# Weight blocks 8 to 11 as two pieces: splitting one step of a float64 unpacking in a Mamba-2 and gated MLP kernel

## The chip, the cores and the metric

The kernel runs on one core of a Trainium2 chip. A core has five engines that run their own instruction streams: TensorE (PE, with its weight loads shown as PEld), VectorE (DVE), ScalarE (ACT), GpSimd (POOL) and SyncE (SP), and 16 DMA engines that move data between HBM and the on-chip memories. The metric is the device time of one execution, in microseconds (us), as the median of several runs.

## What is computed

```python
# attention: batch 4, 8 heads, 768 steps in chunks of 32, head_dim 32, d_state 16
la  = log(clip(a, 1e-6, 1));  cum = cumsum(la) within a chunk
L   = exp(cum[i] - cum[j]) * causal
y   = ((C B^T) * L) x  +  (C state) * exp(cum)
state = exp(sum la) * state + sum_j B_j x_j exp(cum_end - cum_j)
# MLP: 3072 tokens, d_model 256, d_ff 2048; w_in and w_out are float64
h = x @ w_in;  g = h / (1 + exp(-1.702 h));  out = g @ w_out
```

The heads' outputs, side by side, are the tokens of the MLP. All activations are float32. The two weight matrices come as float64, and the chip has no float64 arithmetic, so the kernel turns each word pair into a float32 with integer and float operations on VectorE and ScalarE.

## The kernel before, in words

The 3072 tokens are worked in six groups of 512. For the first group the kernel computes the attention part of two pairs of chunks, then `hidden(0, f)` for the 16 blocks of 128 columns of w_in (line 878), then the projection with w_out in 16 steps (`project_all`, line 976). Later groups use seven-product matrix schemes (lines 934, 944, 1039, 1046), for which VectorE forms sums of weights and of activations.

While the first group runs, the weights are still being loaded and unpacked. `PIECES` (line 155) lists the units of that work: pieces 0 to 3 are two blocks of w_in each (0 and 1, 2 and 3, 4 and 5, 6 and 7), piece 4 is blocks 8 to 11, piece 5 is blocks 12 to 15, and pieces 6 to 9 are four blocks of w_out each. A piece goes through these steps:

- `fetch(i)` (line 164): two DMA transfers on SP into a tile `bits`. Two-block pieces share a tile by twos. There are four such tiles; `NEXT` (line 214) and the schedule say after which join a tile is fetched into again.
- `fields(i)` (lines 193 and 196, VectorE): exponent field `p` and mantissa `m` out of the high words. It waits for the piece's transfers.
- `clamp(i)` (lines 204 and 205, ScalarE): the exponent in float32's range.
- `rounded(i)` (line 209, VectorE): the low word added to the mantissa.
- `join(i, parts)` (lines 223 and 229, VectorE): sign and exponent, then the product into `w_in` or `w_out`. It waits for the clamp. With two parts each half of the piece is done by its own pair of instructions.

`narrow(i)` (line 236) chains these for one piece: `rounded(i)`, then `join(i)` either ahead of `fields(i + 1)` or behind it. `m` and `p` have two buffers each, so at most two pieces are between fields and join.

The order on each engine is the order in which the program is written (`in_order`, line 1409, holds the instructions to it). The table at line 1221 sets behind which hidden block `narrow(i)` and `clamp(i + 1)` are written; `at` (line 1208) adds other work behind hidden blocks or ahead of projection steps: clipping the decays (`store_a` with `az`, line 1213; `clip_rows` with `af`, line 488), `decay_rows` (line 504), the loads of later pairs, `turn` (transposes into a bank `tp`, line 579, and `since_start`, line 649, which multiplies one half of `tp` into `CsT`), and ahead of projection step 10 `score` (line 664) and `gain` (the matmuls A, line 695). PSUM banks come from a ring of four (`bank`, line 563).

Of the kernel before, what the change touches and what calls it, by code (L numbers as in the profile page):

```python
# [35 lines left out]
def kernel(  # L36
# [48 lines left out]
    PG = CG // 2  # L85
# [31 lines left out]
    def load_blocks(p, queues=(nc.sync, nc.sync)):  # L117

        g, n = divmod(p, PG)
        b, c = divmod(2 * p, NC)  # L120
        for queue, name, src in zip(queues, "CB", (C, B)):
            if n == 0:
                blocks[name, g] = raw.tile([P, 2, PG * P], FP32, tag="z", name=f"z{name}{g}", bufs=2)
            for r in range(R):
                queue.dma_start(
                    out=blocks[name, g][32 * r:32 * r + 32, :, n * P:(n + 1) * P],
                    in_=src[b, Q * r:Q * r + Q, c * P:(c + 2) * P].rearrange(
                        "q (i f) n -> i q (f n)", i=32))
# [10 lines left out]
    def load(p, parts=None):  # L139
        if parts is None:  # L140
            parts = "bcx" if p < 2 * PG else "bx"
            if p >= 2 * PG:
                load_blocks(p)
        for part in parts:
            dst, src, e = {"b": (rb, B, N), "c": (rc, C, N), "x": (rx, x, D)}[part]
            dst[p] = raw.tile([P, 2, NH, e], FP32, tag=part, name=f"{part}{p}",
                              bufs=2 if part == "c" else 3)
            for k in range(2):
                b, c = divmod(2 * p + k, NC)
                sl = slice(c * P, (c + 1) * P)  # L150
                nc.sync.dma_start(out=dst[p][:, k], in_=src[b, :, sl, :].rearrange("h s d -> s h d"))


    assert NF == 4 * CG
    PIECES = [("in", f, 2) for f in range(0, 8, 2)] + [("in", 8, 4), ("in", 12, 4)] \
        + [("out", f, 4) for f in range(0, NF, 4)]
    PN = 4 * DM
    BUFS = 4
    bits, pieces = {}, {}

    def words(name):
        return wide.tile([P, 2 * PN], U32, tag="bits", name=name, bufs=BUFS)

    def fetch(i, held=False):
        name, f, n = PIECES[i]
        if n == 2 and f % 4:
            t = pieces.pop(i - 1)[:, 2 * n * DM:]
        else:
            t = pieces[i] = words(f"bits{i}")
            t = t[:, :2 * n * DM]  # L170
        if held:
            held.memset(t[:, :1], 0)
        if name == "in":
            src = moe_w_in[:, 2 * f * P:2 * (f + n) * P].rearrange("(k p) e -> p k e", p=P)
            dst, src = (v.rearrange(s, h=n, e=2 * P) for v, s in (
                (t, "p (h k e) -> k p h e"), (src, "p k (h e) -> k p h e")))
        else:
            src = moe_w_out[f * P:(f + n) * P, :].rearrange("(f p) (h e) -> h p f e", p=P, h=2)
            dst = t.rearrange("p (h f e) -> h p f e", h=2, f=n)
        for k in range(2):  # L180
            nc.sync.dma_start(out=dst[k], in_=src[k])  # L181
        t = t.rearrange("p (e w) -> p e w", w=2)
        bits[i] = t[:, :, 0], t[:, :, 1]
# [3 lines left out]
    mantissa, power = {}, {}  # L187

    def fields(i):
        hi, cols = bits[i][1], slice(0, PIECES[i][2] * DM)  # L190
        mantissa[i] = wide.tile([P, PN], U32, tag="m", name=f"m{i}")[:, cols]
        power[i] = wide.tile([P, PN], U32, tag="p2", name=f"p2{i}")[:, cols]
        nc.vector.tensor_scalar(out=power[i], in0=hi, scalar1=0x7FF00000, scalar2=None,
                                op0=ALU.bitwise_and)

        nc.vector.tensor_scalar(out=mantissa[i], in0=hi, scalar1=0x000FFFFF,
                                scalar2=0x00100000, op0=ALU.bitwise_and, op1=ALU.bitwise_or)

    def clamp(i):


        e = power[i]
        z = e.bitcast(FP32)
        nc.scalar.activation(z, e, AF.Relu, scale=-8.0, bias=edge[:, 0:1])
        nc.scalar.activation(e, z, AF.Relu, scale=-1.0, bias=edge[:, 1:2])

    def rounded(i):

        nc.vector.scalar_tensor_tensor(out=mantissa[i].bitcast(FP32), in0=bits[i][0],
                                       scalar=2.0 ** -32, in1=mantissa[i],  # L210
                                       op0=ALU.mult, op1=ALU.add)


    NEXT = {1: (6,), 5: (9,)}

    def join(i, parts=1):

        name, f, n = PIECES[i]
        n //= parts
        low, m, p2 = bits.pop(i)[1], mantissa.pop(i), power.pop(i)  # L220
        for k in range(parts):
            cols, fs = slice(k * n * DM, (k + 1) * n * DM), slice(f + k * n, f + (k + 1) * n)
            nc.vector.scalar_tensor_tensor(out=p2[:, cols], in0=low[:, cols], scalar=0x80000000,
                                           in1=p2[:, cols], op0=ALU.bitwise_and, op1=ALU.bitwise_or)
            if name == "in":
                dst, h = w_in[:, fs].rearrange("p f k e -> p (f k e)").unsqueeze(1), 1
            else:
                dst, h = w_out[:, :, fs].rearrange("p c f e -> p c (f e)"), 2
            nc.vector.scalar_tensor_tensor(  # L229
                out=dst, in0=m[:, cols].bitcast(FP32).rearrange("p (h e) -> p h e", h=h),  # L230
                scalar=2.0 ** -20, in1=p2[:, cols].bitcast(FP32).rearrange("p (h e) -> p h e", h=h),
                op0=ALU.mult, op1=ALU.mult)
        for n in NEXT.get(i, ()):
            fetch(n)

    def narrow(i):
        rounded(i)
        if i in (2, 4, 5, 6):
            join(i, 2 if i in (4, 5) else 1)
        if i == 6:  # L240
            decay_rows(0)
        if i + 1 < len(PIECES):
            fields(i + 1)
        if i not in (2, 4, 5, 6):
            join(i, 2 if i == 3 else 1)


    scratch = dram.tile([NC, 2, NB * NH, H], FP32, name="scratch")
# [133 lines left out]
    for n in range(PG):  # L382
        t = whose[32 * n:32 * n + 32, n:n + 1]
# [115 lines left out]
    def decay_rows(b):  # L499

        t, first = raf.pop(b), firsts.pop(b)
        if b:
            since[b] = ssd.tile([P, NC, P], FP32, tag="since", name=f"since{b}")
        nc.vector.tensor_tensor_scan(
            out=since[b][:, -t.shape[1]:].rearrange("p c s -> p (c s)"), data0=t.rearrange("p c s -> p (c s)"),
            data1=first.rearrange("p c s -> p (c s)"),
            initial=0.0, op0=ALU.mult, op1=ALU.add)
# [51 lines left out]
    def turn(p):  # L559
        turn_only(p)  # L560
        since_start(p)
# [81 lines left out]
    def since_start(p, engine=nc.vector):  # L643

        b, c = divmod(2 * p, NC)
        s = st[p]
        tp = s["tp"]
        s["CsT"] = ssd.tile([P, 2, P], FP32, tag="CsT", name=f"CsT{p}", bufs=3)
        engine.tensor_tensor(out=s["CsT"], in0=tp, in1=since[b][:, c:c + 2], op=ALU.mult)  # L649
# [79 lines left out]
    def keep_both(pairs, by_scalar=False):  # L729

        for p in pairs:
            part_of(p, range(4), by_scalar)
        for p in pairs:
            add_up(p, range(4))
# [448 lines left out]
    parts_first()  # L1183
    since_start(0, nc.gpsimd)
    fetch(1, held=nc.gpsimd)
    for i in range(2, 6):
        fetch(i)
    nc.sync.dma_start(out=az[:BH].rearrange("p c s -> p (c s)"),
                      in_=a.rearrange("b h s -> (b h) s"))
# [18 lines left out]
    def at(places, i, *work):  # L1208
        places.setdefault(i, []).extend(work)

    in_hidden = [{} for _ in range(NG)]
    in_project = [{} for _ in range(NG)]
    def store_a():
# [1 line left out]
        for i, side in enumerate(SIDES):  # L1215
            nc.sync.dma_start(out=scratch[:, i].rearrange("c r i -> r c i"), in_=az[:BH, :, side])

    at(in_hidden[0], 5, store_a, lambda: fetch(7), lambda: fetch(8),
       lambda: load(PG + 1, "bc"))
    at(in_hidden[0], 8, lambda: clip_rows(0))  # L1220
    for i, k, c in ((2, 1, 1), (3, 2, 2), (4, 4, 7), (5, 8, 10), (6, 10, 14), (7, 14, 15)):
        at(in_hidden[0], k, lambda i=i: narrow(i))
        at(in_hidden[0], c, lambda i=i: clamp(i + 1))
    at(in_hidden[0], 15, lambda: decay_fanned(PG))
# [1 line left out]
       lambda: load(PG, "x"), lambda: load(PG + 1, "x"))  # L1226
    n, p = 2 * PG, 3 * PG
    pairs = PG, PG + 1
    at(in_project[0], 0, lambda: turn(PG), lambda: rounded(8),
       lambda: join(8), lambda: fields(9))  # L1230
    at(in_project[0], 1, lambda: clamp(9))
    at(in_project[0], 2, lambda: clip_rows(1), lambda: decay(PG + 1),
       lambda: decay_rows(1))
    at(in_project[0], 4, lambda: turn(PG + 1))
    at(in_project[0], 5, lambda: narrow(9))
    at(in_project[0], 10, lambda: score(pairs), lambda: gain(pairs), lambda: keep_both(pairs, True),
       lambda: weigh(PG), lambda: weigh(PG + 1))
    at(in_project[0], 15, lambda: finish(pairs))
# [89 lines left out]
    k = NF // 2 - 1  # L1328
# [6 lines left out]
    for g in range(2, NG):  # L1335
        n, p = (g + 1) * PG, (g + 2) * PG
# [60 lines left out]
        k = NF // 2 - 1  # L1397
# [42 lines left out]
```

## Time and profile before

| quantity | value |
|---|---|
| median of 3 runs | 346.89 us (346.83 to 347.21) |
| the profiled execution's own time | 347.67 us |
| its span, first to last instruction of the program | 345.9 us |
| TensorE busy | 339.2 us (98%) |
| VectorE busy | 256.1 us (74%) |
| ScalarE busy | 155.1 us (45%) |
| GpSimd busy | 16.7 us (5%) |
| granted TensorE clock | 1.00 |
| share of the chain that ended last: TensorE, DMA | 92%, 3% |

The busy shares are means over the span. The chain that ended last goes back from the last instruction to whatever released each step. A timeline row gives start, duration, engine, line, operation, output and inputs, shapes and, in brackets, how long the engine stood idle before it and what ended that. "x24" merges 24 instructions in a row. A matmul of 512 columns is two records of 0.43 us each.

The rows of the first 90 us matter here, where the hidden blocks and the projection of the first group run beside the unpacking. Busy time by engine in some stretches:

| stretch, us | length | PE | DVE | ACT | share of the DMA engines |
|---|---|---|---|---|---|
| 24.0 to 29.5 | 5.5 | 4.67 | 4.30 | 3.68 | 1.10 |
| 29.5 to 34 | 4.5 | 4.48 | 4.40 | 3.38 | 0.80 |
| 34 to 42 | 8 | 8.00 | 7.84 | 5.45 | 0.77 |
| 42 to 50 | 8 | 8.00 | 7.40 | 5.97 | 1.00 |
| 50 to 58 | 8 | 8.00 | 7.93 | 2.89 | 1.07 |
| 58 to 66 | 8 | 8.00 | 7.80 | 3.30 | 0.60 |
| 82 to 90 | 8 | 8.00 | 7.14 | 4.55 | 0.54 |

### The profile page before, as it was taken

What the parts mean: (1) busy time and instruction counts of PE and PEld (TensorE: products, weight loads), DVE (VectorE), ACT (ScalarE), POOL (GpSimd) and SP (SyncE); (2) the same over time, 40 slices, a digit from 0 to 9 for tenths busy, and PEclk for the clock granted to TensorE, in tenths of its full rate; (3) what the DMA queues carried; (4) which work ended last, traced back from release to release, by engine and by line L of the source; (5) the groups of instructions that cost most, each with busy time, mean ns of one, the idle gap of its engine ahead of it and who ended that gap; (6) DMA issues with size and microseconds to landing.
All of it is one profiled execution on the core that took longest, in us unless ns stands there. A gap on an engine that the chain in (4) does not pass through costs nothing.

```text
span 345.9 us, 8116 instructions
## 1 busy us (share of the span) xinstructions
PE 339.2 (98%) x3380; PEld 270.2 (78%) x3380; DVE 256.1 (74%) x484; ACT 155.1 (45%) x352; POOL 16.7 (5%) x40
## 2 busy tenths in 40 slices
PE   8999999999999999999999999999999999999996
PEld 6633744555788888888888888888888888899996
DVE  5988999999799998858995667787564654465463
ACT  5786771507454324754332554442454322554320
POOL 7300110300000100000000000000000000000000
PEclk9999999999999999999999999999999999999999
DMA  6698899545637100435603036400000300000401
GB/s 160 132 289 211 217 239 133 152 67 102 122 63 127 36 0 15 65 99 100 110 27 51 2 78 121 64 0 3 0 4 2 62 2 0 0 2 0 63 0 62
DMA packets 90004, 25.76 MB, mean 74 GB/s; under 512 B 73416, under 2 KB 87248, under 8 KB 89968
## 3 DMA queue, kind: packets, MB, share of 16 engines
q1 hardware_dynamic: 89104, 24.72, 35.0%
q10 hardware_dynamic: 832, 0.52, 0.5%
q8 instruction: 26, 0.43, 0.5%
q14 instruction: 10, 0.08, 0.1%
q0 software_dynamic: 32, 0.01, 0.0%
HBM read 22.00 MB, written 3.24 MB: 73 GB/s over the span
## 4 chain that ended last, share of the span: by engine, by line
PE 92%; DMA 3%; SPq 2%; DVE 1%; issue 0%; ACT 0%; POOL 0%; DVEq 0%
PE acc L1039 28%; PE X L934 19%; PE Y L944 14%; PE o L976 8%; PE acc L1046 7%; PE h L878 7%; DMA bits<-in_moe_w_in_dram 3%; PE y L818 2%; PE cb L664 2%; SPq L181 1%; PE y L804 1%; PE A L695 1%; PE ab L536 1%; DMA az<-in_a_dram 1%; POOL CsT L649 0%
## 5 line engine op out<-in xcount | busy, mean ns | idle before, releaser
L939 ACT ACTIVATE ac<-X 128x256 f32<-128x256 f32 x76 | 29.1, 383 | 81.7 <-PE X L934 81.0
L1039 PE MATMUL acc<-mg,mw 128*128 128x256 f32 x192 | 54.5, 379 | 0.0
L1066 DVE TENSOR_TENSOR gT<-Y,ac 128x512 f32<-128x512 f32 x38 | 26.2, 689 | 38.1 <-PE Y L944 32.5
L911 ACT ACTIVATE gT<-gT 128x512 f32<-128x512 f32 (+1 forms) x76 | 38.9, 519 | 29.3 <-DVE gT L1066 28.8
L934 PE MATMUL X<-my,mi 128*128 128x256 f32 x152 | 45.2, 380 | 0.0
L1039 PEld LDWEIGHTS acc<-mg,mw 128*128 128x128 f32 x192 | 36.6, 190 | 4.9
L1066 DVE TENSOR_TENSOR gT<-Y,b 128x256 f32<-128x256 f32 x38 | 15.8, 419 | 28.5 <-PE Y L944 28.5
L878 PE MATMUL h<-yT,w_in 128*128 128x512 f32 (+1 forms) x92 | 35.5, 541 | 1.4 <-DVE w_in L229 0.9
L1039 PE MATMUL acc<-gT,w_out 128*128 128x256 f32 x128 | 35.5, 380 | 0.0
L878 PEld LDWEIGHTS h<-yT,w_in 128*128 128x128 f32 x92 | 17.2, 190 | 18.2 <-issue 12.8
L934 PEld LDWEIGHTS X<-my,mi 128*128 128x128 f32 x152 | 28.0, 190 | 4.0 <-ACT ac L939 0.3
L976 PE MATMUL o<-gT,w_out 128*128 128x512 f32 x64 | 28.3, 596 | 0.0
L902 DVE TENSOR_TENSOR mg<-gT 128x512 f32<-128x512 f32 x40 | 27.2, 681 | 0.0
L1039 PEld LDWEIGHTS acc<-gT,w_out 128*128 128x128 f32 x128 | 24.3, 190 | 3.4 <-ACT yT L853 0.2
L939 ACT ACTIVATE b<-X 128x256 f32<-128x256 f32 x38 | 14.6, 383 | 20.8 <-PE X L934 20.3
L934 PE MATMUL X<-yT,w_in 128*128 128x256 f32 x76 | 23.2, 389 | 0.0
L944 PE MATMUL Y<-yT,w_in 128*128 128x256 f32 x76 | 22.7, 381 | 0.0
L944 PE MATMUL Y<-my,mi 128*128 128x256 f32 x76 | 22.7, 381 | 0.0
L934 PE MATMUL X<-my,w_in 128*128 128x256 f32 x76 | 22.5, 380 | 0.0
L944 PE MATMUL Y<-yT,mi 128*128 128x256 f32 x76 | 22.5, 380 | 0.0
L976 PEld LDWEIGHTS o<-gT,w_out 128*128 128x128 f32 x64 | 11.9, 190 | 13.6 <-issue 12.7
L408 DVE TENSOR_TENSOR_SCAN L<-a,idents 128x1024 f32<-128x1024 f32 x9 | 20.5, 2279 | 0.3 <-DMA a<-scratch 0.3
(152 smaller groups left out, 547.8 us busy)
## 6 DMA issues: line engine op xcount, KB each, us to landing
a<-scratch SPq DMA_DIRECT2D x18, 256.0 KB, 4.9
bits<-in_moe_w_out_dram SPq DMA_DIRECT2D x8, 512.0 KB, 7.4
x<-in_x_dram SPq DMA_DIRECT2D x24, 128.0 KB, 3.7
out_dram<-ob SPq DMA_DIRECT2D x40, 64.0 KB, 2.0
bits<-in_moe_w_in_dram SPq DMA_DIRECT2D x8, 256.0 KB, 3.7
bits<-in_moe_w_in_dram SPq DMA_DIRECT2D x4, 512.0 KB, 11.4
b<-in_B_dram SPq DMA_DIRECT2D x20, 64.0 KB, 3.3
af<-in_a_dram SPq DMA_DIRECT2D x3, 384.0 KB
```

The costliest lines, as they stand in the source:

```text
L408: nc.vector.tensor_tensor_scan(out=L, data0=ra[p].rearrange("p k e -> p (k e)"), data1=idents.rearrange("p h i -> p (h i)"), initial=0.0, ...
L664: nc.tensor.matmul(out=s["cb"][side, r, k].rearrange("p (q i) -> p q i", q=Q), lhsT=BT[rows, k, side], rhs=CT[rows, k, :, side], start=Tru ...
L878: nc.tensor.matmul(out=h[:, cols], lhsT=w_in[:, f, k], rhs=yT[g][:, k, cols], start=(k == 0 and c == 0), stop=(k == NK - 1), skip_group_ch ...
L902: nc.vector.tensor_tensor(out=t[:, 0:2], in0=B[:, :, 1], in1=B[:, 0], op=ALU.subtract)
L911: nc.scalar.activation(o, i, AF.Silu, scale=GELU_SCALE)
L934: nc.tensor.matmul(out=s["X"], lhsT=lhsT, rhs=rhs, start=i == "1", stop=i == "4", skip_group_check=True)
L939: nc.scalar.activation(copy, s["X"], AF.Copy)
L944: nc.tensor.matmul(out=o, lhsT=lhsT, rhs=rhs, start=s.pop("new", False), stop=i != "5", skip_group_check=True)
L976: nc.tensor.matmul(out=o[c], lhsT=w_out[:, c, f], rhs=gT[g, f // 2][:, f % 2], start=(f == 0), stop=(f == NF - 1), skip_group_check=True)
L1039: nc.tensor.matmul(out=acc[g][0][i][:, cols], lhsT=w, rhs=h[:, cols], start=(j == 0 and k == 0 and (i, 0) in begins), stop=(j == NF // 2 - ...
L1046: nc.tensor.matmul(out=o[k] if type(o) is list else o[:, cols], lhsT=h[:, cols], rhs=w, start=(j == 0 and (i, k) in begins), stop=(j == NF ...
L1066: nc.vector.tensor_tensor(out=o, in0=v, in1=w, op=ALU.add)
```

## The change

`PIECES` gets one piece more. Piece 4 is now blocks 8 and 9, piece 5 blocks 10 and 11, piece 6 blocks 12 to 15, pieces 7 to 10 w_out. Pieces 4 and 5 share one tile of `bits`.

`join` gets an argument `only`, which picks some of the parts; the fetch of the next piece goes with the last part. In `narrow(3)` the last step on block 6 (part 0) now stands ahead of `fields(4)` and that on block 7 (part 1) behind it; before, both stood behind. Pieces 4 and 6 are joined in two parts ahead of the next fields, piece 5 in two parts behind them.

The schedule follows: `narrow(4)` is written behind hidden block 3, `narrow(5)` behind 5, `narrow(6)` behind 8, and so on; the clip of `af` now comes behind the join of piece 5, the fetch of the third w_out piece behind that join too. In the built program VectorE has seven instructions more, ScalarE two, SP two transfers; TensorE and GpSimd have the same instructions in the same order.

```diff
-    PIECES = [("in", f, 2) for f in range(0, 8, 2)] + [("in", 8, 4), ("in", 12, 4)] \
+    PIECES = [("in", f, 2) for f in range(0, 12, 2)] + [("in", 12, 4)] \
         + [("out", f, 4) for f in range(0, NF, 4)]
...
-    NEXT = {1: (6,), 5: (9,)}
+    NEXT = {1: (7,), 5: (9,), 6: (10,)}
-    def join(i, parts=1):
+    def join(i, parts=1, only=None):
...
-        for k in range(parts):
+        for k in range(parts) if only is None else only:
...
-        for n in NEXT.get(i, ()):
-            fetch(n)
+        if only is None or parts - 1 in only:
+            for t in bits, mantissa, power:
+                t.pop(i)
+            for n in NEXT.get(i, ()):
+                fetch(n)
     def narrow(i):
         rounded(i)
-        if i in (2, 4, 5, 6):
-            join(i, 2 if i in (4, 5) else 1)
-        if i == 6:
+        if i in (2, 4, 6, 7):
+            join(i, 2 if i in (4, 6) else 1)
+        if i == 7:
             decay_rows(0)
+        if i == 3:
+            join(i, 2, (0,))
         if i + 1 < len(PIECES):
             fields(i + 1)
-        if i not in (2, 4, 5, 6):
-            join(i, 2 if i == 3 else 1)
+        if i == 3:
+            join(i, 2, (1,))
+        elif i not in (2, 4, 6, 7):
+            join(i, 2 if i == 5 else 1)
...
-    for i in range(2, 6):
+    for i in range(2, 7):
         fetch(i)
...
-    at(in_hidden[0], 5, store_a, lambda: fetch(7), lambda: fetch(8),
-       lambda: load(PG + 1, "bc"))
+    at(in_hidden[0], 5, store_a, lambda: fetch(8))
+    at(in_hidden[0], 6, lambda: load(PG + 1, "bc"))
     at(in_hidden[0], 8, lambda: clip_rows(0))
-    for i, k, c in ((2, 1, 1), (3, 2, 2), (4, 4, 7), (5, 8, 10), (6, 10, 14), (7, 14, 15)):
+    for i, k, c in ((2, 1, 1), (3, 2, 2), (4, 3, 5), (5, 5, 7), (6, 8, 10), (7, 10, 14), (8, 14, 15)):
         at(in_hidden[0], k, lambda i=i: narrow(i))
         at(in_hidden[0], c, lambda i=i: clamp(i + 1))
```

The projection's calls (`rounded`, `join`, `fields`, `clamp`, `narrow` of the w_out pieces) only count one higher.

## Prediction

> **What bounds the kernel now.** I read the page's busy shares first (PE 98%), then the waits, the TensorE and VectorE timelines around the one long TensorE wait, and then everything downstream that TensorE takes from VectorE. The PE timeline from 10 to 50 us has these two rows next to each other:
>
> ```profile
> 17.89 10.78 PE L878 MATMUL h<-yT,w_in 128*128 128x512 f32 x24 [0.51 <-ACT yT L838]
> 29.52 17.43 PE L878 MATMUL h<-yT,w_in 128*128 128x512 f32 x52 [0.85 <-DVE w_in L229]
> ```
>
> TensorE computes hidden blocks 0 to 5, stands still, and starts block 6 at 29.52. After that the timeline shows no idle time to the end. Four records of 0.429 us make a block (1.72 us). Block 5's last record starts at 28.07, so block 6 was due at 28.50. Its records are back in step as if it had started at 29.60, so the stall costs 1.09 us. The VectorE timeline says why:
>
> ```profile
> 24.70 0.42 DVE L193 TENSOR_SCALAR p<-bits 128x512 uint32<-128x512 uint32 x1
> 25.03 0.42 DVE L196 TENSOR_SCALAR m<-bits 128x512 uint32<-128x512 uint32 x1
> 25.49 0.69 DVE L209 SCALAR_TENSOR_TENSOR m<-bits,m 128x512 f32<-128x512 uint32 x1
> 27.28 0.69 DVE L193 TENSOR_SCALAR p<-bits 128x1024 uint32<-128x1024 uint32 x1 [1.10 <-DMA bits<-in_moe_w_in_dram]
> 27.89 0.69 DVE L196 TENSOR_SCALAR m<-bits 128x1024 uint32<-128x1024 uint32 x1
> 28.49 0.42 DVE L223 SCALAR_TENSOR_TENSOR p<-bits,p 128x256 uint32<-128x256 uint32 x1
> 28.95 0.43 DVE L229 SCALAR_TENSOR_TENSOR w_in<-m,p 128x256 f32<-128x256 f32 x1
> ```
>
> Block 6's last step (L223, L229) stands behind the fields of piece 4 (L193, L196), and these wait for piece 4's transfer. The chain of waits ends that transfer at 26.76 (17.15 + 9.61). The data for block 6 were there long before.
>
> The second bound lies downstream. VectorE has no slack of its own from 27.28 to 66: in the stretches 34 to 42, 50 to 58 and 58 to 66 us it is busy 7.84, 7.93 and 7.80 of 8 us. TensorE takes something late from it here:
>
> ```profile
> 63.61 1.75 DVE L504 TENSOR_TENSOR_SCAN since<-af,first 128x768 f32<-128x768 f32 x1
> 65.50 0.42 DVE L649 TENSOR_TENSOR CsT<-tp,since 128x256 f32<-128x256 f32 x1
> ```
> ```profile
> 64.93 1.21 PE L664 MATMUL cb<-CT,BT 32*64 32x128 f32 x64
> 66.07 0.79 PE L695 MATMUL A<-x,Be 64*32 64x64 f32 x56
> 66.79 0.70 PE L976 MATMUL o<-gT,w_out 128*128 128x512 f32 x1
> ```
>
> CsT of pair 3 (L649) reads the bank `tp`, and the second matmul of A (L695) writes that bank next. In the built program that matmul waits for exactly this CsT. CsT ends at 65.92 and A begins at 66.07, with the remaining projection steps (L976) queued behind it on TensorE. So TensorE has 0 to 0.1 us to spare here: the handoff from VectorE to a weight load takes 0.05 us (block 2: 21.48 to 21.53) to 0.15 us (block 6: 29.38 to 29.52).
>
> **The change part by part.** All times are of the profiled execution (347.67 us, of which 345.9 is the span).
>
> *The stall.* Piece 3's first half now stands ahead of the next fields. It waits only for ScalarE's clamp of piece 3 (25.91 + 0.72 = 26.63). So L223 starts at 26.66, L229 0.46 later, and block 6 is ready at 27.54, ahead of 28.50. TensorE gains 1.09 us here.
>
> *The pieces.* Piece 4 of four blocks took VectorE 1.21 (L193 and L196, 0.60 each start to start), 1.13 (L209) and 2 x (0.72 + 0.61) = 2.66: 5.00 us. A piece of two blocks takes 2 x 0.336, 0.61, and 2 x (0.46 + 0.34): 2.88, from the 512- and 256-wide rows above. Two of them make 5.76, so the split adds 0.76. The reshuffled clips of `az` and `af` add 0.06 (the memset between them is no longer covered). The Trainium skill, "VectorE: DVE Perf Modes", section on the TRN2 errata, gives each instruction with an SBUF source a fixed 58 cycles. As an estimate, seven more instructions would cost 0.42 us, 0.34 less than the rows say. The rows pay more because half of the new instructions read what the one before them wrote.
>
> *VectorE's clock.* Before: L193 of piece 4 at 27.28, L193 of the first w_out piece at 39.67. After, summed start to start from 26.66: block 6/7 first half 0.80, fields 0.67, second half 0.80, rounded 0.61, join of blocks 8, 9 1.60 (to 31.14), fields 0.67, `az` clip and memset 0.66, rounded 0.61, fields of the last piece 1.20, join of 10, 11 1.60, `af` 0.19, rounded 1.13, join of 12 to 15 2.66. That is 39.87: **0.20 us later than before**. The idle time that goes is 27.28 - 26.66 = 0.62, less than the 0.82 that is added.
>
> *TensorE on the way.* Due 28.50 plus 1.72 per block: block 8 at 31.94 (ready 30.5), block 10 at 35.37 (ready 35.16 plus handoff), block 12 at 38.82 (ready 38.61 plus handoff). The last two are met with nothing to spare. A miss costs 0 to 0.2 us and doesn't matter, since TensorE must wait at A anyway. ScalarE's silu of block 11 stands behind the clamp of the first w_out piece (40.6 to 42.9) and frees its bank at 43.5, ahead of block 15 at 43.96.
>
> *Giving it back.* TensorE would reach A at 66.07 - 1.09 = 64.97. CsT now ends at 65.92 + 0.20 = 66.12, because everything between is VectorE back to back and its one wait there (0.53 at 42.76, for ScalarE's clamp) starts from its own L193. So A begins 0.1 to 0.2 later than before, and the 1.09 becomes a wait of about 1.2 in front of A. From A on nothing in the profile is idle on TensorE, so the shift of A is that of the end: **+0.15 us**.
>
> *Queues.* SP issues the same bytes in the same order, with two more transfers. Piece 5's turn, then the last piece's, then `az`. On SP each new one waits for a transfer eight places back that has landed by then. `fetch` of the third w_out piece now follows the join of piece 5, but SP gets to it only at 36.9 (37.90 before), 1 us after that join. The scratch store can leave when `az` is clipped (31.8 instead of 35.1). POOL's copy behind the `af` clip moves 0.2 us, and its reader stands at 45.16. All of these cost nothing, covered by VectorE's queue. Without cover, a late `az` is the costly one (second rival). Its cost is bounded by 0 and 3.6 us (35.09 - 31.8 plus 0.3).
>
> *Profiled and undisturbed.* The median is 0.78 below the profiled execution. TensorE's stretch after 29.5 runs at 0.429 us per record with a granted clock of 1.00 and leaves no room for that, so the 0.78 lies ahead of 29.5 or outside the span. If some of it lies in the wait for piece 4, the kernel before has less of that idle than 0.62, and the change saves less. The bounds are 0 and 0.78. I take 0.15, near the profiled row. Forecast: 346.89 + 0.15 + 0.15 = **347.2**.
>
> **The rivals.**
>
> *Slower: the wait that goes was shorter than profiled.* Place: L193 of piece 4. Before, the fields of piece 4 fill the time in which the clamp of piece 3 runs (rounded ends at 26.18, clamp at 26.63); after, VectorE idles there. Each 0.1 us by which piece 4 lands earlier than 26.76 makes the kernel before 0.1 faster and the changed one not at all. From a landing at 26.2 the change costs 0.15 + 0.55 = 0.7; at the end of the scale (L193 at 26.10) it costs 1.3. That gives 347.6 to 348.2. For it: the 0.78 has to be somewhere. Against: only this profile exists, and the 1.73 outside the span can hold it.
>
> *Slower: az lands late.* VectorE comes to the `az` clip at 31.81 instead of 35.09. SP's timeline (first fence) has its issue at 20.46 and it took 10.6 us from there, so it landed at 31.07. VectorE starts 0.52 after a landing (26.76 to 27.28), so 31.59: only 0.22 to spare.
>
> ```profile
> 20.46 3.56 SPq L1188 DMA_DIRECT2D az<-in_a_dram  x1
> ```
>
> The DMA view (issues, KB each, median us from issue to landing) shows it beside the pieces:
>
> ```profile
> az<-in_a_dram SPq DMA_DIRECT2D x1, 96.0 KB, 10.6
> bits<-in_moe_w_in_dram SPq DMA_DIRECT2D x8, 256.0 KB, 3.7
> bits<-in_moe_w_in_dram SPq DMA_DIRECT2D x4, 512.0 KB, 11.4
> ```
>
> Every microsecond beyond that is a microsecond at CsT and at the end. If each of the two further transfers held the queue up 0.5 us, the end would be 347.2 + 0.8 = 348.0. Against: the queue is never empty, and back to back transfers hide their starts. The Trainium skill, "DMA: Bandwidth & Descriptors", rules for kernel authors, asks for at least 1 MiB per transfer, and its anatomy section fits 2.0 us plus the bytes to one transfer. As an estimate, by that fixed part `az` would land 4 us later and the time would be near 351. The landings here, 1.5 us apart for two transfers of 512 KB each (25.25 and 26.76), don't show it.
>
> *Faster: A doesn't wait.* If the bank of A were free earlier than I read, the next handoff would be w_out blocks 12 to 15: L229 ends at 69.45 + 0.20, while TensorE would come to it at 70.33 - 1.09 = 69.24. About 0.5 of the 1.09 would stay: 346.4. With VectorE early as well, all of it: 345.8. For it: no view books a wait at A. Against: the built program's wait, and 65.92 beside 66.07.
>
> *The change doesn't do what it says.* Block 6 would be late all the same if ScalarE's clamp of piece 3 were; it ends at 26.63 and nothing new is ahead of it. Then the end moves by the same +0.2 at A.
>
> **How the numbers follow.** Forecast 0.45 (347.2, its own range 346.8 to 347.5); first slower rival 0.28 (347.6 to 348.2); late `az` 0.10 (348.0); faster 0.14 (345.8 to 346.4); no effect at block 6 0.03 (347.1). The range 346.4 to 348.1 holds the forecast, most of the first slower rival and the edge of the faster one. 0.2% is 0.69 us, about what a measurement of this kernel can tell from no change. Faster than 346.2: 0.12. Slower than 347.6: 0.38, from both slower rivals. The rest, 0.50, is within it.
>
> **What would show it.** Right: no TensorE idle ahead of block 6; VectorE's first w_out L193 at 39.9; CsT's end later than 65.92; a TensorE gap of about 1 us ahead of A, or of the projection step just behind it. Wrong: A starting a microsecond earlier than 66.07 with TensorE busy from block 6 on; an idle VectorE ahead of the `az` clip (second rival); TensorE's row at block 6 starting later than 28.6.

## The result, and the profile after

| | kernel before | changed kernel |
|---|---|---|
| median | 347.05 us (346.50 to 347.98, 8 runs) | 348.32 us (347.95 to 349.14, 8 runs) |
| ratio of the runs | | 1.0039 [1.0024, 1.0053] |
| profiled execution, span | 347.67 us, 345.9 us | 349.14 us, 347.4 us |

The changed kernel is 1.27 us (0.4%) slower. The forecast was 347.2, the range 346.4 to 348.1: wrong, on the slow side. Four executions of the experiments below, at 352.31, 358.41, 706.70 and 1988.01 us, ran in a slow state and are left out of the medians, so that a gain given here as 0.32 stands as 0.34 in one expectation.

The TensorE timeline of the changed kernel, with the two places that answer to the rows shown of before (the line numbers are seven higher):

```profile
19.34 27.76 PE L885 MATMUL h<-yT,w_in 128*128 128x512 f32 x76 [0.51 <-ACT yT L845]
...
65.08 1.21 PE L671 MATMUL cb<-CT,BT 32*64 32x128 f32 x64
66.22 0.30 PE L702 MATMUL A<-x,Be 64*32 64x64 f32 x2
67.24 0.77 PE L702 MATMUL A<-x,Be 64*32 64x64 f32 x54 [0.73 <-DVE CsT L656]
```

All hidden blocks (76 records) are one row now: the stall at block 6 is gone. In its place TensorE stands still inside A, behind its second matmul, and the profile names the releaser that the built program had shown: CsT. The VectorE timeline:

```profile
25.87 0.42 DVE L193 TENSOR_SCALAR p<-bits 128x512 uint32<-128x512 uint32 x1
26.20 0.42 DVE L196 TENSOR_SCALAR m<-bits 128x512 uint32<-128x512 uint32 x1
26.66 0.69 DVE L209 SCALAR_TENSOR_TENSOR m<-bits,m 128x512 f32<-128x512 uint32 x1
27.83 0.42 DVE L223 SCALAR_TENSOR_TENSOR p<-bits,p 128x256 uint32<-128x256 uint32 x1 [0.48 <-ACT p L205]
28.29 0.42 DVE L229 SCALAR_TENSOR_TENSOR w_in<-m,p 128x256 f32<-128x256 f32 x1
28.63 0.42 DVE L193 TENSOR_SCALAR p<-bits 128x512 uint32<-128x512 uint32 x1
...
64.88 1.75 DVE L511 TENSOR_TENSOR_SCAN since<-af,first 128x768 f32<-128x768 f32 x1
66.76 0.42 DVE L656 TENSOR_TENSOR CsT<-tp,since 128x256 f32<-128x256 f32 x1
...
107.83 2.29 DVE L415 TENSOR_TENSOR_SCAN L<-a,idents 128x1024 f32<-128x1024 f32 x1 [0.64 <-DMA zB<-in_B_dram]
```

VectorE no longer waits for a transfer ahead of piece 4's fields; it waits 0.48 for ScalarE's clamp of piece 3. The last row is far from the change, and the prediction had not looked there: a scan that needs a transfer. The scan reads `a`, which two loads of 256 KB (`a<-scratch`, below called the spread) bring in, one behind the other. The profile puts this wait down to another load of the same queue; the second load of the spread landed at 107.74, 0.09 ahead of the scan. The kernel before has the wait too, but shorter:

```profile
106.26 2.29 DVE L408 TENSOR_TENSOR_SCAN L<-a,idents 128x1024 f32<-128x1024 f32 x1 [0.32 <-DMA a<-scratch]
```

In every profile but those with earlier spreads, VectorE is ready for this scan 5.3 to 5.4 us behind the issue of the spread; a spread that takes longer makes it wait. The view of waits of the changed kernel shows both ends of the story on TensorE, the second 50 us behind the first:

```profile
PE A L702 <- DVE CsT L656: 0.7, 1, 0.7
PE X L941 <- ACT ac L946: 0.3, 1, 0.3
```

Clock readings of the two profiles can't be subtracted as they stand. In this execution the first loads of x came late (the first landed at 11.47; in the eight profiles with the usual start that show it, at 9.6 to 9.9), and everything is 1.2 us later before the change has begun: L193 of piece 3 starts at 25.87, not 24.70. Of 15 further profiles 13 have that row at 24.63 to 24.92, one at 25.47 and one at 26.77. The 25.47 is the changed kernel again, so both of its profiles start late; four kernels that differ from it only behind 50 us start at 24.75 to 24.92. So the change does not force a late start, but how often the changed kernel has one is not known. Counted from that row, A's third matmul stands at 67.24 - 25.87 = 41.37 in the changed kernel and at 41.37 in the kernel before (first matmul 66.07, no gap behind it). **Against the profiled execution of before, the change costs nothing at A.** So the question is what is usual, and what is lost behind A.

### The profile page after: what moved, and what is told of

Same layout as the page of the kernel before. It is cut to its first block, busy times and chain, and to the rows that moved or that the text cites. A ratio compares the mean times of both kernels' runs of the same rounds, so it can differ in the third digit from the quotient of the medians.

```text
span 347.4 us, 8131 instructions
## 1 busy us (share of the span) xinstructions
PE 340.4 (98%) x3380; PEld 270.8 (78%) x3380; DVE 256.7 (74%) x491; ACT 155.5 (45%) x354; POOL 16.8 (5%) x40
## 4 chain that ended last, share of the span: by engine, by line
PE 86%; DVE 6%; DMA 4%; SPq 2%; issue 1%; POOL 0%; ACT 0%; DVEq 0%; POOLq 0%
PE acc L1046 25%; PE X L941 17%; PE Y L951 13%; PE h L885 10%; PE acc L1053 7%; PE o L983 5%; PE y L825 2%; PE cb L671 2%; PE y L811 1%; PE A L702 1%; DMA bits<-in_moe_w_in_dram 1%; DVE L L415 1%; DMA x<-in_x_dram 1%; DVE mw L1006 1%; SPq L125 1%
```

## The experiments

Two things differ from what the prediction took: how long VectorE waits for piece 4 in a usual execution of the kernel before, and whether the way from A to the end is free. Kernels measured together ran on one chip, with the kernel before beside them. A gain or loss below is the difference of the two medians; the interval is that of the ratio.

**The kernel before, again** (no edit).

> The kernel before, unchanged, profiled once more. Both theories: a time within 0.3 us of the kernel before. Theory W (the wait for piece 4 belongs to the one profiled execution, and most runs don't have it): VectorE's fields of piece 4 (L193, 1024 wide) start less than 2.0 us behind those of piece 3 (2.58 in the first profile), and the idle time ahead of them shrinks from 1.10 towards 0. Theory S (the wait is always there, and the changed kernel lost its time at a later start, which its one more transfer brings): again about 2.6 us between the two and 1.1 idle, and hidden block 0 again at 17.9 and not at 19.3.

Measured: 347.36 beside 347.05, [1.0003, 1.0025]. The same kernel differs from itself by 0.31 us, so a difference of that size between two medians says little by itself, and the traces have to carry the reading.

```profile
24.80 0.42 DVE L193 TENSOR_SCALAR p<-bits 128x512 uint32<-128x512 uint32 x1
...
26.94 0.69 DVE L193 TENSOR_SCALAR p<-bits 128x1024 uint32<-128x1024 uint32 x1 [0.65 <-DMA bits<-in_moe_w_in_dram]
```

The wait is there again, but 0.65 instead of 1.10, and this execution took 347.13 instead of 347.67. Neither theory had it right: it is neither always 1.1 nor absent. The start is at 17.8, as theory S had it for this kernel.

**The order alone.**

```diff
+        if i == 3:
+            join(i, 2, (0,))
         if i + 1 < len(PIECES):
             fields(i + 1)
+        if i == 3:
+            join(i, 2, (1,))
```

> The order alone: pieces as before (blocks 8 to 11 in one piece), only the last step on block 6 and 7 stands ahead of the fields of piece 4, and only its second half behind them. Nothing is added on VectorE or on SP. Theory W: VectorE idles 0.45 to 0.6 us for ScalarE's clamp, which the fields covered; the end moves by +0.4 to +0.6 us. Theory S: the wait for piece 4 is still there but now covers the first half (0.8 us of work), VectorE gets 0.6 to 0.8 ahead, A comes as much earlier as TensorE allows: -0.5 to -0.8 us.

Measured: 347.67 beside 347.05, [1.0009, 1.0048]. Its profiled execution is disturbed from 84 us on (351.05 us, waits for loads of x), so only its first part is read. TensorE timeline, block 6 starting on time and then:

```profile
31.12 15.75 PE L885 MATMUL h<-yT,w_in 128*128 128x512 f32 x48 [0.66 <-ACT gT L889]
```

The stall moved one block on: block 7 now waits, for ScalarE, and `tp` begins at 46.71, no earlier than in the two profiles of before (46.79, 46.45). What the order alone wins at block 6 is gone before the projection begins. Theory S's gain of 0.5 to 0.8 did not come; the loss of 0.62 is theory W's in size, but half of it is what the kernel before differs from itself.

**The pieces alone**: the changed kernel with both halves of the last step on blocks 6 and 7 behind `fields(4)`.

```diff
-        if i == 3:
-            join(i, 2, (0,))
         if i + 1 < len(PIECES):
             fields(i + 1)
-        if i == 3:
-            join(i, 2, (1,))
-        elif i not in (2, 4, 6, 7):
-            join(i, 2 if i == 5 else 1)
+        if i not in (2, 4, 6, 7):
+            join(i, 2 if i in (3, 5) else 1)
```

> The pieces alone: as the changed kernel, but the fields of piece 4 (two blocks) stand ahead of both halves of the last step on blocks 6 and 7, as before. Theory W: +0.8 us (the 0.76 of the split and the 0.06 of the clips), no idle time waiting for the clamp beyond 0.1. Theory S: the start comes 1.2 to 1.45 us later as in the changed kernel's trace, and the end +0.9 to +1.4, while the interval from piece 3's L193 to CsT's end is below 41.2 us.

Measured: 347.61 beside 347.05, [1.0004, 1.0035]. The start was the usual one (hidden block 0 at 18.23), which theory S had at 19.3: the late start is not the transfers' doing. Counted from L193 of piece 3, A stands at 40.77, **0.60 earlier** than with the new order, because the fields of piece 4 again fill the time of the clamp. What was won there was lost later, on VectorE near 106 and on TensorE near 117:

```profile
106.43 2.29 DVE L411 TENSOR_TENSOR_SCAN L<-a,idents 128x1024 f32<-128x1024 f32 x1 [0.97 <-DMA a<-scratch]
```
```profile
PE X L937 <- ACT ac L942: 0.3, 1, 0.3
```

**More work ahead of piece 4's fields**, in the kernel before: two ANDs in place, the values unchanged.

```diff
+        if i == 3:
+            for _ in range(2):
+                nc.vector.tensor_scalar(out=mantissa[3], in0=mantissa[3], scalar1=0x7FFFFFFF,
+                                        scalar2=None, op0=ALU.bitwise_and)
         if i + 1 < len(PIECES):
             fields(i + 1)
```

> The kernel before with two more VectorE instructions (an AND over 128x512 words in place, leaving the values as they are) between L209 of piece 3 and the fields of piece 4, about 1.0 to 1.2 us of VectorE time by the spacing of L209. Theory W: there is no wait to cover them, so the end moves by +0.9 to +1.2 us. Theory S: they lie in the wait of 1.10 us, and the end moves by 0 to +0.2 us.

Measured: 347.39 beside 347.05, [1.0005, 1.0046]; the kernel before itself had 347.36 on that chip.

```profile
26.16 0.89 DVE L244 TENSOR_SCALAR m<-m 128x512 uint32<-128x512 uint32 x2
26.97 0.69 DVE L193 TENSOR_SCALAR p<-bits 128x1024 uint32<-128x1024 uint32 x1
```

With two more instructions (26.16 to 26.97) piece 4's fields start 2.32 us behind those of piece 3, only 0.18 later than in the profile above (2.14). Mostly covered, then, as theory S had it; yet in this very execution piece 4 landed at 25.20, so here there was no wait to cover them. Piece 4's last transfer lands at 26.76 (before), 26.42 (again), 26.25 (the order alone) and 25.20 (here). Theory W and theory S both fall as they stood: the wait varies from nothing to 1.1.

**The transfers alone**: the kernel before, piece 4 loaded by four transfers of 256 KB.

```diff
-        for k in range(2):
-            nc.sync.dma_start(out=dst[k], in_=src[k])
+        for half in (slice(0, 2), slice(2, 4)) if (name, f) == ("in", 8) else (slice(0, n),):
+            for k in range(2):
...
+                    nc.sync.dma_start(out=dst[k][:, half], in_=src[k][:, half])
```

> The kernel before with the two transfers of piece 4 (512 KB each) cut into four of 256 KB, as in the changed kernel; pieces, VectorE and order as before. Theory P: two more transfers shift every later one by two places in the queue, and there a pause of 0.4 to 0.9 us opens between the two spreads of a (a<-scratch, near 104 us), VectorE's scan that waits for the second one (L408 of before, near 106) starts that much later, and the end moves by +0.3 to +0.8 us. Theory V (all that was lost was lost on VectorE between 26 and 66 us; the pause in two of the six traces is chance): 0 within 0.3 us.

Measured: 346.46 beside 346.78, [0.9967, 1.0006]; run again on another chip 346.71 beside 347.12, [0.9974, 1.0007] (below). VectorE and TensorE timelines:

```profile
24.75 0.42 DVE L197 TENSOR_SCALAR p<-bits 128x512 uint32<-128x512 uint32 x1
...
26.14 0.69 DVE L197 TENSOR_SCALAR p<-bits 128x1024 uint32<-128x1024 uint32 x1
```
```profile
18.16 27.76 PE L882 MATMUL h<-yT,w_in 128*128 128x512 f32 x76 [0.51 <-ACT yT L842]
...
65.03 0.79 PE L699 MATMUL A<-x,Be 64*32 64x64 f32 x56
```

This is the kernel before without the wait: piece 4's last transfer landed at 24.80. The stall at block 6 is gone without a single VectorE instruction moved, and A stands at 40.28. It is the reference that the prediction lacked. From it: each 0.1 us of wait is about 0.1 us at CsT (its end 40.01 behind piece 3's L193 without a wait, 40.76 with 0.65, 41.22 with 1.10).

**VectorE alone**: the changed kernel with pieces 4 and 5 loaded by before's two transfers of 512 KB.

```diff
+        if (name, f) == ("in", 10):
+            t = pieces.pop(i - 1)[:, 2 * n * DM:].rearrange("p (e w) -> p e w", w=2)
+            bits[i] = t[:, :, 0], t[:, :, 1]
+            return
+        if (name, f) == ("in", 8):
+            t = pieces[i] = words(f"bits{i}")
+            n = 4
```

> The changed kernel with pieces 4 and 5 loaded together by the kernel before's own two transfers of 512 KB: the queue as before, VectorE's instructions and order as in the changed kernel. Theory P: no pause between the two spreads, A late by 0.3 to 0.6 us against a usual run of the kernel before, the end +0.4 to +0.8 us. Theory V: as the changed kernel, +1.1 to +1.3 us.

Measured: 347.97 beside 346.78, [1.0001, 1.0041]. A stands at 41.31, as in the changed kernel, and the scan waits 0.35. By its time it speaks for theory V; by its trace, half of what the changed kernel loses at the scan was lost here too. With before's own transfers the loss is 1.19, so the two more transfers are not needed for most of it.

**The spreads earlier**: the changed kernel, with the loads near 100 us written one step of mixing earlier.

```diff
-    for j in range(2):
-        mix_g(1, j)
+    mix_g(1, 0)
     more_loads()
+    mix_g(1, 1)
```

> The changed kernel with the spreads near 100 us (and the loads of B and C between them) issued one step of mixing (about 1.5 us of VectorE) earlier. Nothing ahead of 98 us is touched. Theory P: the scan near 106 us no longer waits for the spread; against the kernel before +0.5 to +0.8 us instead of +1.2. Theory V: +1.1 to +1.3 us, as the changed kernel.

Measured: 347.46 beside 346.78, [0.9986, 1.0030], a loss of 0.68. TensorE's and VectorE's rows:

```profile
66.23 0.78 PE L702 MATMUL A<-x,Be 64*32 64x64 f32 x54 [0.78 <-DVE CsT L656]
```
```profile
106.01 2.28 DVE L415 TENSOR_TENSOR_SCAN L<-a,idents 128x1024 f32<-128x1024 f32 x1
```

The gap ahead of A stays, the wait ahead of the scan is gone, and so is half of the loss, as theory P had it. The interval reaches from a gain to a loss of 1.0, below the 1.1 of theory V.

**A freed from CsT**: the changed kernel, pair 3's transposed C copied out of its bank by ScalarE.

```diff
-        if 2 in steps and p < PG:
+        if 2 in steps and p == PG + 1:
             tp = s["tp"]
-            s["tp"] = ssd.tile([P, 2, P], FP32, tag="CsT", name=f"C{p}", bufs=3)
+            s["tp"] = ssd.tile([P, TG], FP32, tag="Ct", name=f"C{p}", bufs=1)[...]
```

> The changed kernel with pair 3's transposed C copied out of its bank by ScalarE, as a fourth copy behind BT and CT, so that A's bank no longer waits for CsT (L656) on VectorE. Both theories: no TensorE gap ahead of A, A starts where cb ends, 0.4 to 1.0 us earlier than in the changed kernel; the next handoff (w_out blocks 12 to 15) takes 0.3 to 0.5 of it back. Against the kernel before: theory P +0.3 to +0.6 us (the pause stays), theory V -0.1 to -0.4 us. If A does not come earlier, the bank was not what held it.

Measured: 347.37 beside 346.78, [0.9988, 1.0024], a loss of 0.59. Theory P had +0.3 to +0.6; the interval still reaches down to theory V's gain.

```profile
65.08 0.81 PE L703 MATMUL A<-x,Be 64*32 64x64 f32 x56
```
```profile
106.09 2.29 DVE L415 TENSOR_TENSOR_SCAN L<-a,idents 128x1024 f32<-128x1024 f32 x1 [0.72 <-DMA a<-scratch]
```

A stands at 40.28, as in the transfers-only kernel, though CsT ends as late as before (41.27). The bank was what held A. The scan's wait is untouched.

**The changed kernel again** (no edit), with three more on one chip.

> The changed kernel, unchanged, beside the others on one chip, and profiled once more. Theory two-part (A late by VectorE's added time, 0.5 to 0.8 us against a usual run of the kernel before, and the scan near 106 us late by a spread that lands 5.6 to 6.3 us behind its issue, 0.3 to 0.9 us): start at 17.8 to 18.3 and not 19.3, CsT's end at 66.0 to 66.2, the spread again over 5.6 us, +1.0 to +1.3 us. Theory V (VectorE alone): the same total, the spread at 5.3 us, and no wait ahead of the scan.

Measured: 348.35 beside 347.05, [1.0002, 1.0051], again +1.3. A at 41.36, the spread 5.96 us behind its issue, a wait at both places, as the two-part theory had it. Its start was not as expected: hidden block 0 at 18.47 and piece 3's L193 at 25.47, some 0.7 later than usual, and with it CsT's end at 66.77.

```profile
66.83 0.78 PE L702 MATMUL A<-x,Be 64*32 64x64 f32 x54 [0.61 <-DVE CsT L656]
```
```profile
107.31 2.29 DVE L415 TENSOR_TENSOR_SCAN L<-a,idents 128x1024 f32<-128x1024 f32 x1 [0.66 <-DMA a<-scratch]
```

**More work without the wait**: the transfers-only kernel with the two ANDs of above.

> The kernel before with the transfers of piece 4 cut as in the queue-only run (its VectorE did not wait for piece 4), and two more VectorE instructions (AND in place over 128x512 words, 0.81 us together in the trace of e4_more_ahead) ahead of the fields of piece 4. If VectorE without that wait has no slack down to A: against the queue-only run +0.4 to +0.8 us (TensorE has 0.2 to 0.3 us to spare at A there), against the kernel before +0.1 to +0.5. If VectorE has slack elsewhere: as the queue-only run, -0.3 us against the kernel before.

Measured: 347.48 beside 347.05, [0.9983, 1.0037]; a loss of 0.43, which against the transfers-only kernel's -0.32 and -0.41 makes 0.75 to 0.84. The two instructions move piece 4's fields by 0.92 (2.32 behind piece 3's instead of 1.40) and CsT's end by 0.93; A stands at 41.10 instead of 40.28, 0.82 later. Where VectorE doesn't wait, nearly all of its work goes to A; how much of the loss is the scan's, which waits 0.52 in this profile, is not separated.

**The transfers cut and the spreads earlier**, the kernel before otherwise.

> The kernel before with the transfers of piece 4 cut in two, and the spreads near 100 us one step of mixing earlier. No VectorE instruction is added. Theory two-part: no TensorE idle at block 6 (28.6), at A or near 116, in every execution: -0.3 to -0.6 us against the kernel before, lowest run at or below 346.2. Theory V: as the queue-only run, -0.3 us.

Measured: 346.64 beside 347.05, [0.9959, 1.0017], lowest run 346.32: a gain of 0.41, like that of the cut transfers alone, and not resolved, so the medians do not show whether earlier spreads bring anything here. Its profiled execution began 2 us late. Counted from piece 3's L193 it took 319.8 us to the end, as the transfers-only kernel's first profile, whose scan hardly waits (319.8); the second, whose scan waits 0.43, took 320.1.

**Both handoffs opened** in the changed kernel: the copy on ScalarE and the earlier spreads.

> The changed kernel with both of its late handoffs opened: A's bank freed by a copy on ScalarE, and the spreads near 100 us one step of mixing earlier. Theory two-part: both losses go, against the kernel before -0.3 to +0.1 us (A comes on time at 65.1; what is left is the handoff of w_out blocks 12 to 15). Theory V: +0.1 to +0.5 us, as e8_A_free at its best.

Measured: 347.08 beside 347.05, [0.9968, 1.0016]. By the median the whole loss is gone. On this chip 11 of its 12 runs are faster than the fastest of the changed kernel (347.95). Theory V had +0.1 to +0.5, which the interval does not exclude; neither wait is left in the trace:

```profile
65.25 0.81 PE L703 MATMUL A<-x,Be 64*32 64x64 f32 x56
```
```profile
105.35 2.28 DVE L415 TENSOR_TENSOR_SCAN L<-a,idents 128x1024 f32<-128x1024 f32 x1
```

The profiles side by side (us; A and CsT's end counted from L193 of piece 3; the spread from the issue of the first of the two transfers to the landing of the second; the last column from L193 of piece 3 to the end of the span, which leaves out a late start):

| kernel | its time | idle ahead of piece 4's fields | A | CsT's end | spread | idle ahead of the scan | L193 to the end |
|---|---|---|---|---|---|---|---|
| before | 347.67 | 1.10 | 41.37 | 41.22 | 5.61 | 0.32 | 321.2 |
| before, again | 347.13 | 0.65 | 40.92 | 40.76 | 5.33 | 0 | 320.6 |
| transfers alone | 346.29 | 0 | 40.28 | 40.01 | 5.35 | 0 | 319.8 |
| transfers alone, again | 346.58 | 0 | 40.28 | 39.99 | 5.72 | 0.43 | 320.1 |
| more work without the wait | 347.40 | 0 | 41.10 | 40.94 | 5.82 | 0.52 | 321.0 |
| pieces alone | 347.70 | 0 | 40.77 | 40.71 | 6.27 | 0.97 | 321.2 |
| VectorE alone | 347.83 | 0 | 41.31 | 41.25 | 5.64 | 0.35 | 321.3 |
| changed | 349.14 | 0 | 41.37 | 41.32 | 5.94 | 0.64 | 321.5 |
| changed, again | 348.61 | 0 | 41.36 | 41.31 | 5.96 | 0.66 | 321.4 |
| spreads earlier | 347.51 | 0 | 41.36 | 41.30 | 5.56 | 0 | 320.9 |
| A freed | 347.37 | 0 | 40.28 | 41.27 | 6.02 | 0.72 | 320.8 |
| both opened | 346.83 | 0 | 40.33 | 41.25 | 5.30 | 0 | 320.2 |

**Why the spread lands late.** With the changed pieces and the cut transfers it took 5.94 to 6.27 us in four of four profiles. The DMA engines' busy tenths in 40 slices from 102 to 107 us, first the kernel with A freed, then the transfers-only kernel:

```profile
DMA  9987659797878400014455688998655200000001
```
```profile
DMA  5679959865675879998633553000004510158999
```

In the first all engines are all but idle for three slices (some 0.4 us) ahead of the second transfer's packets; in the second they are idle only behind its landing (104.83). Three more kernels asked whether it is the place in SP's queue of transfers, which two more transfers shift: six or two transfers of 1 KB were added behind the loads near 50 us.

```diff
+    def extra():
+        for i in range(6):
+            nc.sync.dma_start(out=dram.tile([P, 2], FP32, name=f"extra{i}"), in_=edge)
+
+    at(in_project[0], 4, extra)
```

> The changed kernel with six more transfers of 1 KB (a constant, written to memory that nothing reads) on SP behind the loads near 50 us, so that from there on every transfer has the place modulo eight in the queue that it has in the kernel before. Theory place (the late spread near 104 us comes from the places that two more transfers shift): no pause, the spread lands 5.2 to 5.6 us behind its issue, A late as before: +0.6 to +0.8 us against the kernel before. Theory other (not the place): 5.9 to 6.3 us and +1.2 to +1.3 us, as the changed kernel.

> The kernel before with two such transfers of 1 KB at the same spot, so that the later transfers have the changed kernel's places. Pieces, VectorE and the loads up to 50 us as before. Theory place: the spread lands 5.8 to 6.3 us behind its issue, +0.3 to +0.6 us. Theory other: 5.2 to 5.6 us, 0 within 0.2 us.

> The queue-only kernel once more (transfers of piece 4 cut in two, nothing else), beside these two on one chip. Theory place: the early landing of its first profile was chance, now 5.8 us or more, and its gain of 0.34 holds the loss already. Theory other: again 5.3 to 5.4 us. Both: no TensorE idle at block 6, -0.2 to -0.5 us against the kernel before.

Measured: the changed kernel with the old places 350.28 beside 347.12, [1.0072, 1.0125]. It answers nothing: the added transfers delayed the next loads and opened waits in A of the next group, near 84 us (the first two rows of the view of waits; the third is the known one).

```profile
PE A L702 <- DMA x<-in_x_dram: 1.3, 2, 0.8
PE A L702 <- DVE Be L478: 1.2, 1, 1.2
PE A L702 <- DVE CsT L656: 0.8, 1, 0.8
```

The kernel before with the new places: 347.57 beside 347.12, [0.9997, 1.0027]; the spread landed at 5.85 and the scan waited 0.56, but the loads of x were late here too (0.46 at A). The transfers-only kernel again: 346.71 beside 347.12, [0.9974, 1.0007]; the spread landed at 5.72. So with the old places (before twice, the order alone, the ANDs, VectorE alone) it takes 5.24 to 5.64 us (5.72 in the kernel that answers nothing), and with the new ones, the earlier-spread kernels left out, 5.35, 5.72, 5.82, 5.85, 5.94, 5.96, 6.02 and 6.27. That leans to theory place. The 5.35, and the transfers-only kernel's time, which shows no loss on either chip, speak against it as the whole cause. **It stays open.**

## Why the prediction was wrong, step by step

- *The stall*: right. Block 6 starts on time and TensorE's 1.09 us is gone from that place.
- *The pieces*: right in size. From the clamp (27.83) to the first w_out piece's L193 (40.95 in the trace) it took 13.12 us; the sum had 13.21. The pieces alone bring CsT from 40.01 to 40.71, +0.70 where 0.82 was summed. The estimate by the Trainium skill ("VectorE: DVE Perf Modes", the TRN2 errata: 58 cycles for each added instruction, 0.42 us) is too small for that. The prediction's reason for the difference holds, but for two of the seven new instructions and not half of them: behind L223 the next start comes after 0.46 us, since L229 reads what L223 wrote, and behind L229 after 0.34 (27.83, 28.29, 28.63 above). That is 0.12 us for each of the two added pairs.
- *VectorE's clock*: right against the profiled execution. The first w_out L193 stands 15.08 behind piece 3's L193 (14.97 before): +0.11, forecast +0.20. CsT's end: 41.32 to 41.22, +0.10. Against a kernel that doesn't wait for piece 4 it is +1.31: 40.01, then 0.70 for the pieces (40.71), then 0.61 for the order, by which VectorE waits for ScalarE's clamp (0.48 in the row above; 41.32).
- *TensorE on the way*: right; one row from 19.34 to `tp`.
- *Giving it back*: the mechanism was right and was shown: CsT holds A by its bank, and with the bank freed A comes 1.1 earlier (40.28). A's third matmul follows its first by 0.91 to 1.08 us in three profiles (66.22 to 67.24, 65.15 to 66.23, 65.92 to 66.83); forecast was a wait of about 1.2. **The last sentence of this step failed**: "from A on nothing in the profile is idle on TensorE, so the shift of A is that of the end". That was true of TensorE and not of VectorE: a scan near 106 waits for a spread (0.32 in the very trace of before), and TensorE's X near 116 comes late behind it. Without that wait the changed kernel is 0.6 us faster (+1.27 against +0.68 with earlier spreads).
- *Queues*: half right. `az` was in time (its clip starts at 32.97 without a wait), so the second rival did not happen: `az` landed at 29.52, 8.8 us behind its issue, where the sum took 10.6, and the 4 us that the prediction estimated by the Trainium skill ("DMA: Bandwidth & Descriptors", anatomy) did not show. That page's 2.0 us is fitted to transfers issued by GpSimd, and these are issued by SP. Cutting the transfers cost nothing; piece 4 even landed earlier. That they move every later transfer was counted as nothing, and may not be nothing: the open question above.
- *Profiled and undisturbed*: **the main failure**, a mis-sized term. The prediction put 0.15 of the 0.78 us between the profiled and the usual time of before into the wait for piece 4, "near the profiled row". The profiles of the kernel before and of its transfers-only twin, which differ mainly in that wait, run 346.29 and 346.58 (none), 347.13 (0.65) and 347.67 (1.10); 346.58 and 347.67 also hold a wait at the scan. By them the median of 347.05 belongs to a wait of about 0.55 (347.05 less some 346.5); the plain runs have no trace that would show it. So most of the 0.78 sits there. The saving is 0.55 less than the profile shows, and A comes later by about that against a usual run: 41.36 against 40.28 + 0.55, some 0.5. By the runs, freeing A is worth 0.7 (1.27 less 0.59).
- The first rival named this mechanism and place, and 347.6 to 348.2, with a chance of 0.28. Its argument "the 0.78 has to be somewhere" was the right one. The measured 348.32 lies 0.1 above its range; by the traces it is that rival, at the wait of a usual run, plus the spread.

What opening the two places is worth adds up: 0.7 at A and 0.6 at the spread, 1.3 together, and both opened give +0.03. The last column of the table says the same without the starts: 0.6 to 0.7, 0.5 to 0.6 and 1.2 to 1.3. Not all of that was lost there. The freed A (40.28) stands earlier than in the kernel before (40.92 and 41.37), and the kernel before waits for the spread too in one of its two profiles. By the traces the loss against a usual run of before is about 0.5 at A and 0.4 behind it, 0.9 together, which is also what the fastest run of the changed kernel loses (347.95 to 347.05). The other 0.4 is not explained. The late starts of both profiles of the changed kernel are a candidate that no run tests, and the kernel before differs from itself by 0.31.

The change was aimed at the right wait from the wrong side. The wait came from a transfer that landed late, and loading the same piece by smaller transfers removes it with no VectorE work at all. With the transfers-only kernel the wait was gone in both profiles. It is the fastest found (-0.32 and -0.41 on two chips), though each of its intervals still holds 1.

## What to carry to other kernels

A wait in one profiled execution is a sample. When the plain runs are faster than the profiled one, look first for the difference in the wait that the change is to remove, and price the change with the wait at zero. Behind the last handoff that one has followed, look at the other engines' waits for transfers too: an engine without idle time can be about to have some. And ask of a wait for a transfer whether the transfer can come earlier, before work is cut up to go around it.

## What the runs showed of the hardware

- Cutting two transfers of 512 KB into four of 256 KB brought the same 1 MB in at 24.66 to 25.13 us (three profiles) instead of 25.20 to 27.02 (six), with the transfers ahead of it unchanged. The Trainium skill ("DMA: Bandwidth & Descriptors", rules for kernel authors) asks for larger transfers; in this queue of many transfers smaller ones landed earlier. The five kernels with the changed pieces and the usual start have the same four transfers in at 23.98 to 24.99.
- The landing of a transfer behind a full queue varied by 1.56 us (25.20 to 26.76) between executions of the same loads; the kernel before's time with a wait of 0.65 and of 1.10 differed by 0.54.
- Two dependent ANDs over 128x512 words cost VectorE 0.92 us (piece 4's fields 2.32 instead of 1.40 behind piece 3's), and 0.82 of it reached A where VectorE had no wait.
- An instruction that reads what the one before it wrote starts 0.12 us later than one that doesn't: 0.46 instead of 0.34 us behind a start over 128x256 words.
- Six transfers of 1 KB each, which nothing reads, made a kernel 1.9 us slower (3.16 less the changed kernel's 1.27); its trace shows loads of x behind them that came late.
